# A seven-product feed-forward stage: order of the products and bank copies, GpSimd's subtractions on VectorE, the second group's weights converted ahead through DRAM, conversion steps paced

## The chip, the core and the metric

One NeuronCore of a Trainium2 chip runs the whole program. The metric is the device time of one execution in microseconds; the median of three runs of the kernel before is 1168.42 us.

TensorE (PE) multiplies into eight PSUM banks. VectorE (DVE), ScalarE (ACT) and GpSimd (POOL) do the elementwise work, SyncE (SP) issues the DMAs. Each engine takes its instructions in the order of its own queue, and one that waits holds those behind it.

## The reference

The program chains an attention layer, a gated feed-forward layer and a second feed-forward layer. The change lies in the third:

```python
def _moe2_ref(x, w_in, w_out):          # x: 2304 x 512, w_in: 512 x 2048, w_out: 2048 x 512
    h = np.maximum(x @ w_in, 0.0)
    return (h * h @ w_out).astype(np.float32)

def reference(**kwargs):
    ...
    attn_out = _attn_ref(**attn_kwargs)
    ...
    x = _moe_ref(x=x, **moe_kwargs)     # silu(x @ w_gate) * (x @ w_val) @ w_out, d_ff = 1536
    return _moe2_ref(x=x, **moe2_kwargs)
```

The weights reach the kernel as 64-bit floating-point words. Every operand of a matmul is split into a high part (a copy in the type `fp32r`) and a low part (the difference), and every product is the sum of three matmuls: high by high, high by low, low by high.

## The kernel before

**Stages.** Attention and most of the first feed-forward layer (MoE 1) fill the first 650 us. MoE 1's third group of four f-blocks (`steps2`, `idx == 2`) then runs over five blocks of tokens, four of 512 columns and one of 256. MoE 2 (`steps3`) is last. It has four groups of four f-blocks (`G2`), and each group runs over three sub-blocks `sb` of 768 tokens.

**A sub-block of MoE 2.** `first2` computes the hidden values of one sub-block, `second2` multiplies them by the output weights and adds them into `acc`. `first2` uses a seven-product scheme for two-by-two block matrices: the seven left factors in `LEFT` are sums of blocks of `w_in`, the seven right factors in `FACTORS` are sums of blocks of x. For each of the seven, the two pairs `pr` of f-blocks get six matmuls of 384 columns each, so a product has 12 matmuls. The products accumulate in three pairs of PSUM banks: `A` (mm0, mm1), `Bk` (mm2, mm3) and `C` (mm4, mm5). The line

```python
bank = (A, Bk, A, C, A, A, C)[k][pr][:, :BK]
```

gives the pair of product k. A bank that goes on accumulating is copied out in between: `take` (ScalarE, L1307) copies it into one of three buffers h, `plus` (VectorE, L1310) adds a bank to such a buffer. The next product into the same bank can start only when that read is done. `squares` makes relu(h) squared and splits it into the two halves `u` which `second2` (L1373) reads; on ScalarE that is two instructions (L1298, L1299), on VectorE one (L1296). `second2` runs 72 matmuls of 512 columns.

**The right factors.** `Right2` makes seven factors for each sub-block in five slots of 128 x 1536 elements, ahead of their use. In the first group they are made from x (L1235 subtracts on GpSimd; L53 and L61 are the helpers that make the high copy on ScalarE and the low difference on VectorE), and the four that are sums (`T1` to `T4`) are also stored in DRAM. The later groups load those four and make `11`, `21` and `22` again.

**The weights.** `Weights2` converts the weights of a group. A piece of 128 x 256 words is fetched by SP into one of two buffers `wr`; then come one ScalarE instruction (`absolute`, L1031), four VectorE instructions on integers and floats (L1042, L1045, L1052, L1034), and for each result a high copy on ScalarE (L53) and a low difference on VectorE (L61). The four left factors that are sums take four more VectorE instructions (L1080). A group has 16 pieces, 22 splits and 8 sums. The results go to areas of 128 x 512 ("grains") taken from the list `free`; grains come back when a group's weights were read for the last time. The first group is converted while MoE 1's third group runs, the others each during the group ahead of it.

**What sets the order.** Nothing is ordered by hand on the chip. The generators yield after some matmuls, and `go` then hands out pending copies (`flush`), one step of `Right2` and, by a budget for each engine, some steps of `Weights2` (`turn`). The framework's scheduler takes the instructions in about this order and may move one ahead of another on the same engine.

The names in the rows: `mm` are PSUM banks, `right` and part of `wa` are the slots of the right factors, the rest of `wa` and `wb` hold weights, `wf` and `wr` are the conversion's buffers, `ub` and `wx` hold u, `sum` the sums of `Right2`, `xF` the output sums, `x` is x2.

Of the kernel before, what the change touches and what calls it, by code (L numbers as in the profile page):

```python
# [19 lines left out]
P = 128  # L20
# [47 lines left out]
def attention_moe(tc, qkv, qk0, tau, w1, w2, out, cfg):  # L68
# [902 lines left out]
    class Weights2:  # L971


        def __init__(self):
# [3 lines left out]
            self.raws = {}  # L978
            self.n = 0
            self.used = 0  # L980
            self.turns = 0
            self.touched = {}
            self.fl = [loader.bufs[0][1], loader.bufs[1][1], wf3]
            self.win = {}
            self.wout = {}
            self.left = {}

        def group(self, g):
            for j in range(2):
                f = 4 * g + 2 * j  # L990
                self.wait.append(("in", (g, j), f, 7))
            for j in range(4):
                self.wait.append(("out", (g, j), 4 * g + j, 2))

        def more(self):
            while self.wait and len(self.steps) < 24 and len(free) >= self.wait[0][3]:
                kind, key, f, n = self.wait.popleft()
                area = [free.popleft() for _ in range(n)]
                if kind == "in":
                    self.win[key] = dict(zip(("11", "12", "22", "S1", "S2", "S3", "S4"), area))  # L1000
                    self.pair(key, f)
                else:
                    self.wout[key] = area
                    self.out(key, f)
                self.left[kind, key] = len(self.steps)
# [4 lines left out]
        def fetch(self):  # L1010
            while self.n < self.used + 2 and self.pieces:
                f, c0 = self.pieces.popleft()
                raw = loader.bufs[self.n % 2][0]
                nc.sync.dma_start(raw, w2[f, :, c0 : c0 + PIECE])
                self.n += 1

        def conv(self, f, c0, j):
# [22 lines left out]
            a = ("A", absolute, (j,))  # L1040
# [29 lines left out]
        def pair(self, key, f):  # L1070
            w = self.win[key]

            def sp(j, name):
                return self.split(j, w[name][:, :PIECE], w[name][:, PIECE:], name)
# [27 lines left out]
        def out(self, key, f):  # L1102
            hi, lo = self.wout[key]
            j = 1 + f % 2
            for c in (0, PIECE):
                a, d = self.conv(f, DM + c, j)
                h, l = self.split(j, hi[:, c : c + PIECE], lo[:, c : c + PIECE], "o")
                self.steps += [a, *d, h, l]
                j = 0

        def turn(self):
            self.more()
            self.turns += 1
            budget = {"A": 1, "D": 1 + (self.turns % 4 == 0), "P": 1}
            while self.steps:
                eng, fn, touch = self.steps[0]
                if not budget[eng] or any(
# [5 lines left out]
                budget[eng] -= 1  # L1123

        def emit(self):
            eng, fn, touch = self.steps.popleft()
            for x in touch:
                self.touched[x] = (eng, self.turns)
            fn()

        def until(self, kind, key):
            while any((k, key_) == (kind, key) for k, key_, *_ in self.wait):
                self.more()
                if self.steps:
# [423 lines left out]
```

## Time and profile before

| | |
|---|---|
| median of three runs | 1168.42 us (1167.64 to 1168.72) |
| the profiled execution | 1168.47 us, its span 1166.7 us |
| PE busy | 1120.5 us (96%) |
| weight loads (PEld) busy | 1012.1 us (87%) |
| DVE, ACT, POOL busy | 862.3, 730.1, 268.9 us |
| DMA | 122.19 MB, mean 105 GB/s |

The span runs from the first to the last instruction of the core; 1.77 us of the profiled execution lie around it. Busy times are sums over the whole span, in which stages with different limits follow each other, so the share of an engine says little about one stage. A row of the timeline gives the start of a run of equal instructions, its length, and in brackets how long the engine sat idle ahead of it and which instruction ended that. A row of busy time by stretch gives the stretch, its length, the busy time (and count of instructions) of PE, PEld, DVE, ACT and POOL, then PEclk, the DMA engines' mean busy share and GB/s. The column PEclk gives the granted clock of TensorE as a share of its full 2.4 GHz.

### The profile page before, as it was taken

The numbers are of one execution on the slowest core, as the hardware profiler recorded it, in microseconds if no ns is written. First come the engines' busy times: TensorE is split into PE (matmuls) and PEld (weight loads), VectorE is DVE, ScalarE is ACT, GpSimd is POOL, SyncE is SP. The second block draws the span as 40 slices with busy tenths as digits, with TensorE's granted clock in tenths as the row PEclk, the third lists the DMA queues.
The fourth block names the chain that finished last, engine by engine and source line by source line (L and its number), as shares of the span: only waits on it lengthen the run. The fifth ranks groups of instructions, "written<-read, shape, count | busy, mean of one in ns | idle before, by whom it ended". The sixth has DMA issues, their size and how long they took to land. (4 is left out here: it accounts for less than half of the span.)

```text
span 1166.7 us, 19585 instructions
## 1 busy us (share of the span) xinstructions
PE 1120.5 (96%) x6572; PEld 1012.1 (87%) x6572; DVE 862.3 (74%) x2078; ACT 730.1 (63%) x1734; POOL 268.9 (23%) x377
## 2 busy tenths in 40 slices
PE   6888999999999999999999999989999999999998
PEld 5776989899999999988888888888798898898887
DVE  7999997877777764889976854687678767856443
ACT  7998888988888873555434321255667655655443
POOL 5565664555464521000000000042100000000000
PEclk9999999999999999999999999999999999999999
DMA  6665433344343300233210110133344444333441
GB/s 201 198 167 161 129 101 92 91 119 103 91 115 94 96 2 25 94 91 91 73 56 10 65 36 1 37 117 127 126 145 164 152 136 138 125 120 124 163 163 55
DMA packets 47765, 122.19 MB, mean 105 GB/s; under 512 B 6704, under 2 KB 7984, under 8 KB 47664
## 3 DMA queue, kind: packets, MB, share of 16 engines
q1 hardware_dynamic: 47520, 120.94, 34.4%
q8 instruction: 52, 0.85, 0.3%
q14 instruction: 49, 0.40, 0.1%
q10 hardware_dynamic: 144, 0.00, 0.0%
HBM read 80.22 MB, written 14.16 MB: 81 GB/s over the span
## 5 line engine op out<-in xcount | busy, mean ns | idle before, releaser
L669 PE MATMUL bank<-ident,e 128*128 128x128 f32 x720 | 165.5, 275 | 10.1 <-ACT x L53 3.8
L649 POOL TENSOR_SCALAR e<-e,r 128x576 f32<-128x576 f32 x144 | 113.9, 791 | 147.4 <-DVE r L644 100.9
L61 DVE TENSOR_TENSOR pt<-bank,pt 128x384 fp32r<-128x384 f32 x216 | 100.3, 486 | 51.1 <-ACT pt L689 49.7
L226 PE MATMUL mm<-xs,wa 128*128 128x512 f32 (+2 forms) x672 | 125.8, 347 | 0.5 <-ACT x L53 0.5
L631 ACT ACTIVATE z<-s,thr 128x576 f32<-128x576 f32 x144 | 106.9, 742 | 26.3 <-DVE st__101 L623 18.5
L226 PEld LDWEIGHTS mm<-xs,wa 128*128 128x128 f32 x672 | 109.5, 188 | 15.7 <-ACT x L53 0.7
L623 DVE TENSOR_SCALAR_CACHE_REDUCE st__101<-s,tau_c 128x576 bf16<-128x576 f32 x144 | 116.5, 809 | 4.9 <-PE s L613 3.7
L669 PEld LDWEIGHTS bank<-ident,e 128*128 128x128 f32 x720 | 96.3, 141 | 21.9 <-DVE x L55 5.6
L226 PE MATMUL bank<-xs_m,wa 128*128 128x288 f32 x576 | 109.7, 327 | 3.9 <-DVE xF L740 1.8
L689 ACT ACTIVATE pt<-bank 128x384 fp32r<-128x384 f32 x216 | 88.8, 437 | 21.5 <-PE bank L669 20.2
L639 ACT ACTIVATE e<-z 128x577 f32<-128x577 f32 x144 | 99.6, 691 | 1.5 <-POOL e L649 0.4
L226 PEld LDWEIGHTS bank<-xs_m,wa 128*128 128x128 f32 x576 | 88.9, 189 | 7.3 <-DVE xs_m L61 2.9
L728 PE MATMUL bank<-pt,vs 128*128 128x256 f32 (+1 forms) x480 | 92.2, 323 | 2.1 <-ACT pt L689 1.4
L613 PE MATMUL s<-kh,qs 128*128 128x288 f32 x256 | 78.1, 319 | 7.4 <-ACT nident L413 5.9
L1235 POOL TENSOR_TENSOR sum<-x 128x768 f32<-128x768 f32 x4 | 7.9, 1971 | 315.4 <-DVE wx L61 309.9
L1373 PE MATMUL mm<-wb,ub 128*128 128x512 f32 x324 | 79.4, 394 | 0.0
L1322 PE MATMUL mm<-right,wb 128*128 128x384 f32 x348 | 70.5, 352 | 8.4 <-ACT h L1307 5.0
L728 PEld LDWEIGHTS bank<-pt,vs 128*128 128x128 f32 x480 | 74.0, 190 | 3.9 <-ACT pt L689 2.2
L226 PE MATMUL mm<-xs,wb 128*128 128x512 f32 (+1 forms) x360 | 74.9, 368 | 0.0
L1322 PEld LDWEIGHTS mm<-right,wb 128*128 128x128 f32 x348 | 64.2, 199 | 11.3 <-ACT h L1307 6.6
L613 PE MATMUL s<-kl,qs 128*128 128x288 f32 x256 | 73.7, 301 | 0.0
L226 PEld LDWEIGHTS mm<-xs,wb 128*128 128x128 f32 x360 | 62.8, 188 | 11.3
(157 smaller groups left out, 2602.4 us busy)
## 6 DMA issues: line engine op xcount, KB each, us to landing
wr<-in_w_dram SPq DMA_DIRECT2D x106, 256.0 KB, 3.0
raw<-in_qkv_dram SPq DMA_DIRECT2D x15, 896.0 KB, 4.6
kh<-land SPq DMA_DIRECT2D x60, 144.0 KB, 2.6
kl<-raw SPq DMA_DIRECT2D x60, 144.0 KB, 2.8
xF<-in_w_dram SPq DMA_DIRECT2D x30, 256.0 KB, 3.0
right<-kept0T SPq DMA_DIRECT2D x8, 768.0 KB, 5.4
right<-kept1T SPq DMA_DIRECT2D x7, 768.0 KB, 4.3
right<-kept2T SPq DMA_DIRECT2D x7, 768.0 KB, 5.1
```

What stands on the lines that cost most here:

```text
L61: e.tensor_tensor(out, a, b, op=ALU.subtract)
L226: mm(pt[:, :n], w[:, a, col + c * P : col + (c + 1) * P], xs[:, b, c, :], start=(i == 0), stop=(i == len(TERMS) - 1),)
L613: mm(sp[:, cols], l, r[:, cols], start=(n_ == 0), stop=(n_ == len(pairs) - 1),)
L623: red = nc.vector.tensor_scalar(st_, st[t]["s"][:, :S], scalar1=tau_c, scalar2=None, op0=ALU.subtract, op1=ALU.max, accum_out=th)
L631: nc.scalar.activation(z[:, :S], st[t]["s"][:, :S], AF.Prelu, bias=st[t]["thr"], scale=-1.0, alpha=1 / SLOPE)
L639: ex = nc.scalar.activation(e, st[t]["z"], AF.Exp, scale=-SLOPE, accum_out=sum_)
L649: nc.gpsimd.tensor_scalar(e, e, scalar1=r, scalar2=1.0, op0=ALU.mult, op1=ALU.mult)
L669: mm(dst[:, j], e[:, c0 : c0 + P], ident, is_transpose=True, start=(j == 0), stop=(j == len(cols) - 1),)
L689: nc.scalar.activation(pt[:, s0 : s0 + n, o : o + P], src, AF.Copy)
L728: mm(o[:, :n], hd["vs"][:, SLOT[k % 5], :], pt[:, k, lo : lo + n], start=(k == 0), stop=(k == 9))
L1322: mm(bank, w[:, a, c * P : (c + 1) * P], t[:, b, c, :], start=(n == 0 and x in ("11", "12", "S1")), stop=(n == 5), skip_group_check=x not ...
L1373: mm(pt, u[:, b, s * P : (s + 1) * P], w[a], start=(half == 0 and j == 0 and i == 0), stop=(half == 1 and j == 1 and i == 2),)
```

## The change

1. **Order of products.** The sixth and seventh product change places: `S4` by `22` comes sixth, `22` by `T4` seventh. The banks become A, Bk, A, C, A, C, A. The fourth product (`S1`, bank C) is now copied out by ScalarE, and the fifth (`S3`, bank A) is added to that copy by VectorE; before, it was the other way round. `second2` takes the second half of the token blocks first.
2. **Bank reads early.** `take`, `plus` and the relu reads of a bank are handed to the scheduler with a priority 60 places ahead.
3. **GpSimd idle.** The subtractions of `Right2` run on VectorE.
4. **Squares.** `sq2` chooses the engine by group: VectorE for both pairs in the first and last group, ScalarE in the two between (before: one pair on each in the first group, ScalarE in the rest).
5. **Fifth kept factor.** `22` is stored and loaded again like `T1` to `T4`.
6. **Second group's weights ahead.** All of them are converted right behind the first group's left factors, during MoE 1's third group, into four grains used in turn (`bounce`), stored to DRAM from there, and later loaded into their places.
7. **Pace.** VectorE steps of `Weights2` are handed out by a credit per turn (0.95 in MoE 1, then 0.45 to 1.0) in place of 1.25; the piece behind the current one is fetched as soon as its buffer is free; a piece's first ScalarE step waits 4 turns (8 in MoE 2) from its fetch; freed grains are handed on 8 turns later; `until` flushes no more steps than it needs.

The core of the diff:

```diff
+            ahead = [("ahead in", (1, j), 4 + 2 * j, 0) for j in range(2)]
+            ahead += [("ahead out", (1, j), 4 + j, 0) for j in range(4)]
+            self.wait += left + (ahead + [("given", (1, 0), 0, 0)] if g == 0 else []) + outs
...
+                if kind in ("in", "out") and key[0] == 1:
+                    for x, to in self.win[key].items() if kind == "in" else enumerate(area):
+                        src = keptw[kind, key[1], x]
+                        self.step("S", lambda to=to, src=src: nc.sync.dma_start(to.bitcast(F32), src))
...
+        def store(self, step, to, name):
+            def f():
+                step[1]()
+                nc.sync.dma_start(keptw[name], to.bitcast(F32))
...
-            budget = {"A": 1, "D": 1 + (self.turns % 4 == 0), "P": 1}
+            self.credit = min(self.credit + self.rate, 2)
+            budget = {"A": 1, "D": int(self.credit), "S": 2}
+            while self.later and self.later[0][0] <= self.turns:
+                free.extend(self.later.popleft()[1])
+            self.fetch()
...
+                if raw and self.turns < self.fetched.get(raw[0], self.turns) + self.land:
+                    break
...
-                        free.extend(wbg)
+                        weights2.bounce = deque(wbg[:4])
+                        free.extend(wbg[4:])
...
-    FACTORS = ("11", "21", "T2", "T1", "T3", "T4", "22")
-    LEFT = ("11", "12", "S2", "S1", "S3", "22", "S4")
+    FACTORS = ("11", "21", "T2", "T1", "T3", "22", "T4")
+    KEPT = ("T1", "T2", "T3", "T4", "22")
...
-                        eng.tensor_tensor(out[:, :, c], u, w, op=ALU.subtract)
-
-                return (e, f)
+                        nc.vector.tensor_tensor(out[:, :, c], u, w, op=ALU.subtract)
+
+                return ("D", f)
...
-            e = "DA"[pr] if g == 0 else "A"
+            e = cfg["sq2"][g][pr]
...
+        def read(f, bank):
+            def g_():
+                with tc.high_priority(offset=cfg["soon"]):
+                    f()
+                unread[id(bank)] -= 1
...
-                bank = (A, Bk, A, C, A, A, C)[k][pr][:, :BK]
+                bank = (A, Bk, A, C, A, C, A)[k][pr]
...
                 elif x == "S1":
-                    post = []
+                    post = [take(h[2], bank)]
                 elif x == "S3":
-                    post = [take(h[2], bank), plus(h[2], C[pr][:, :BK]), *squares(pr, 1, 1, h[2])]
+                    post = [plus(h[2], bank), *squares(pr, 1, 1, h[2])]
...
+        order = [*range(nb, 2 * nb), *range(nb)]
...
-                        free.extend(weights2.win[g, pr].values())
+                        weights2.freed(weights2.win[g, pr].values())
...
-    "ta": "P",
+    "sq2": ("DD", "AA", "AA", "DD"),
+    "soon": 60,
+    "pace": (0.95, 0.45, 0.85, 0.55, 1.0),
```

TensorE's queue in the first sub-block of the first group, from the fourth product to the start of `second2` (L1322 and L1381 are `first2`, L1434 is `second2`; the banks are mm0 and mm1 for A, mm4 and mm5 for C). Before:

```order
L1322 MATMUL mm4_6025<-wa_69,wb_5996 128x384 x6
L1322 MATMUL mm5_6026<-wa_69,wb_5996 128x384 x6
L1322 MATMUL mm0_6021<-wa_69,wb_5996 128x384 x6
L1322 MATMUL mm1_6022<-wa_69,wb_5996 128x384 x6
L1322 MATMUL mm0_6021<-right0_8521,wb_5996 128x384 x6
L1322 MATMUL mm1_6022<-right0_8521,wb_5996 128x384 x6
L1322 MATMUL mm4_6025<-right1_8522,wb_5996 128x384 x6
L1322 MATMUL mm5_6026<-right1_8522,wb_5996 128x384 x6
L1373 MATMUL mm6_6027<-wb_5996,ub_6012 128x512 x6
```

Now:

```order
L1381 MATMUL mm4_6025<-wa_69,wb_5996 128x384 x6
L1381 MATMUL mm5_6026<-wa_69,wb_5996 128x384 x6
L1381 MATMUL mm0_6021<-wa_69,wb_5996 128x384 x6
L1381 MATMUL mm1_6022<-wa_69,wb_5996 128x384 x6
L1381 MATMUL mm4_6025<-right0_8671,wb_5996 128x384 x6
L1381 MATMUL mm5_6026<-right0_8671,wb_5996 128x384 x6
L1381 MATMUL mm0_6021<-right1_8672,wb_5996 128x384 x6
L1381 MATMUL mm1_6022<-right1_8672,wb_5996 128x384 x6
L1434 MATMUL mm3_6024<-wa_69,ub_6012 128x512 x3
L1381 MATMUL mm0_6021<-right2_8673,wb_5996 128x384 x6
L1381 MATMUL mm1_6022<-right2_8673,wb_5996 128x384 x6
```

Between two products into mm0 there now always lie 12 matmuls or more into other banks. Three matmuls of `second2` are followed by the next sub-block's first product.

ScalarE's queue around the first `take` of the second sub-block (`h00` from mm0; L1031 is a piece's first conversion step, `wa` from `wf` a weight's high copy). Before:

```order
L53 ACTIVATE xF_64<-mm3_6024 128x512
L1031 ACTIVATE wf22_6004<-wr0_6000 128x256
L53 ACTIVATE wa_69<-wf22_6004 128x256 x2
L53 ACTIVATE xF_64<-mm6_6027 128x512
L53 ACTIVATE wa_69<-wf21_6003 128x256
L53 ACTIVATE xF_64<-mm7_6028 128x512
L1031 ACTIVATE wf20_6001<-wr1_6002 128x256
L53 ACTIVATE wa_69<-wf21_6003 128x256
L1307 ACTIVATE h00_8526<-mm0_6021 128x384
L1307 ACTIVATE h10_8529<-mm1_6022 128x384
```

Now (L1365 is `take`):

```order
L53 ACTIVATE wx_73<-h11_8680 128x384
L53 ACTIVATE ub_6012<-h00_8676 128x384
L53 ACTIVATE right1_8672<-sum0_8674 128x768
L1365 ACTIVATE h00_8676<-mm0_6021 128x384
L53 ACTIVATE wx_73<-h10_8679 128x384
L53 ACTIVATE xF_64<-mm6_6027 128x512
L53 ACTIVATE xF_64<-mm7_6028 128x512
L1365 ACTIVATE h10_8679<-mm1_6022 128x384
L53 ACTIVATE xF_64<-mm2_6023 128x512
```

The conversion's instructions ahead of the `take` are gone, and the `take` stands ahead of the outputs' copies (`xF`).

VectorE's queue at the start of MoE 2 (L286 adds MoE 1's last outputs into `x2b`, L1042 to L1034 are conversion steps, `right` and `wa` from `x2` or `sum` are right factors). Before:

```order
L286 TENSOR_TENSOR x2b_6008<-x2b_6008,mm0_6021 128x256
L61 TENSOR_TENSOR right2_8523<-sum1_8525,right2_8523 128x768
L61 TENSOR_TENSOR wa_69<-wf20_6001,wa_69 128x256
L286 TENSOR_TENSOR x2b_6008<-x2b_6008,mm1_6022 128x256
L61 TENSOR_TENSOR wa_69<-sum0_8524,wa_69 128x768
L1042 TENSOR_SCALAR wf20_6001<-wf20_6001 128x256
L61 TENSOR_TENSOR wa_69<-wf21_6003,wa_69 128x256
L1045 TENSOR_SCALAR wf20_6001<-wf20_6001 128x256
L1052 SCALAR_TENSOR_TENSOR wf20_6001<-wr1_6002,wf20_6001 128x256
L1034 SCALAR_TENSOR_TENSOR wf20_6001<-wr1_6002,wf20_6001 128x256
L1310 TENSOR_TENSOR h00_8526<-mm2_6023,h00_8526 128x384
L61 TENSOR_TENSOR wa_69<-sum0_8524,wa_69 128x768
```

Now (L1281 are the subtractions that GpSimd did, L1368 is `plus`):

```order
L61 TENSOR_TENSOR right0_8671<-x2_65,right0_8671 128x768
L61 TENSOR_TENSOR right1_8672<-x2_65,right1_8672 128x768
L1281 TENSOR_TENSOR sum1_8675<-x2_65,sum0_8674 128x768
L286 TENSOR_TENSOR x2b_6008<-x2b_6008,mm7_6028 128x256
L286 TENSOR_TENSOR x2b_6008<-x2b_6008,mm0_6021 128x256
L286 TENSOR_TENSOR x2b_6008<-x2b_6008,mm1_6022 128x256
L61 TENSOR_TENSOR right2_8673<-sum1_8675,right2_8673 128x768
L61 TENSOR_TENSOR wa_69<-sum0_8674,wa_69 128x768
L1281 TENSOR_TENSOR sum1_8675<-x2_65,sum1_8675 128x768
L1368 TENSOR_TENSOR h00_8676<-mm2_6023,h00_8676 128x384
L1281 TENSOR_TENSOR sum0_8674<-x2_65 128x768
L1368 TENSOR_TENSOR h10_8679<-mm3_6024,h10_8679 128x384
```

Conversion steps have left this place, and subtractions have come.

## Rows read from the trace of the kernel before

**Rows 1.** Busy us (count) by stretch, columns as above: MoE 2's groups, 100 us of MoE 1

```profile
768.94:874.87 105.93, 99.41 (x468) 88.50 (x469) 80.92 (x153) 64.23 (x135) 21.39 (x12) 0.95 0.40 142
874.87:972.82 97.95, 94.55 (x469) 83.93 (x468) 71.65 (x167) 59.98 (x143) 0.00 (x0) 1.00 0.42 142
972.82:1069.35 96.53, 94.12 (x469) 83.98 (x468) 71.51 (x165) 58.09 (x138) 0.00 (x0) 1.00 0.40 137
1069.35:1162.52 93.17, 93.13 (x469) 83.88 (x467) 41.14 (x69) 44.33 (x99) 0.00 (x0) 1.00 0.35 122
660.00:760.00 100.00, 100.00 (x483) 84.56 (x482) 56.20 (x123) 25.93 (x55) 0.00 (x0) 1.00 0.09 30
```

**Rows 2.** Chain of waits (start, length, engine, line): both halves of one sub-block

```profile
1038.35 14.58 PE mm L1322 x84
1052.93 16.58 PE mm L1373 x72
```

**Rows 3.** Who PE waited for from 766 us on: total us, times, longest

```profile
PE mm L1322 <- ACT h L1307: 10.5, 11, 1.5
PE mm L1322 <- DVE h L1310: 1.7, 1, 1.7
PE mm L1322 <- ACT wa L53: 1.5, 1, 1.5
```

**Rows 4.** Timeline of PE: three waits in three groups

```profile
786.17 3.56 PE L1322 MATMUL mm<-right,wb 128*128 128x384 f32 x12 [1.73 <-DVE h L1310]
...
821.86 3.78 PE L1322 MATMUL mm<-right,wb 128*128 128x384 f32 x12 [1.51 <-ACT h L1307]
...
1017.54 2.38 PE L1322 MATMUL mm<-wa,wb 128*128 128x384 f32 x12 [0.69 <-ACT h L1307]
```

**Rows 5.** Three stretches: length, PE busy (count), PEclk, DMA share, GB/s

```profile
770.00:780.00 10.00, 9.87 (x48) 0.83 0.59 236
780.00:790.00 10.00, 7.78 (x36) 0.87 0.34 105
...
820.00:830.00 10.00, 8.49 (x37) 0.83 0.20 79
```

**Rows 6.** Who ACT waited for from 766 us on

```profile
ACT wf L1031 <- DMA wr<-in_w_dram: 31.3, 16, 3.6
ACT wb L53 <- DVE wf L1034: 15.5, 11, 2.1
```

**Rows 7.** Timeline of POOL, one subtraction

```profile
769.74 1.94 POOL L1235 TENSOR_TENSOR sum<-x,sum 128x768 f32<-128x768 f32 x1 [2.42 <-DVE right L61]
```

**Rows 8.** Timeline of DVE, one instruction beside it and three later

```profile
770.25 2.25 DVE L61 TENSOR_TENSOR wa<-sum,wa 128x768 fp32r<-128x768 f32 x1
...
783.37 0.94 DVE L61 TENSOR_TENSOR right<-x,right 128x768 fp32r<-128x768 f32 x1
784.24 0.54 DVE L61 TENSOR_TENSOR wx<-h,wx 128x384 fp32r<-128x384 f32 x1
784.71 0.94 DVE L61 TENSOR_TENSOR wa<-x,wa 128x768 fp32r<-128x768 f32 x1
```

**Rows 9.** Groups (count | busy, mean ns | idle) of DVE, 640 us on

```profile
L1052 DVE SCALAR_TENSOR_TENSOR wf<-wr,wf 128x256 int32<-128x256 int32 x60 | 24.8, 422 | 1.0
...
L61 DVE TENSOR_TENSOR wb<-wf,wb 128x256 fp32r<-128x256 f32 x45 | 18.9, 422 | 14.4 <-PE mm L1322 8.4 <-ACT wb L53 5.6
...
L1042 DVE TENSOR_SCALAR wf<-wf 128x256 f32<-128x256 f32 x58 | 16.3, 290 | 27.6 <-ACT wf L1031 27.3
```

**Rows 10.** Group of ACT, same stretch: the conversion's high copies

```profile
L53 ACT ACTIVATE wb<-wf 128x256 fp32r<-128x256 f32 x45 | 18.5, 414 | 38.1 <-DVE wf L1034 23.0 <-PE mm L1322 11.4 <-DVE wf L1080 3.6
```

**Rows 11.** DMA issues, same stretch: count, KB each, median us to landing

```profile
wr<-in_w_dram SPq DMA_DIRECT2D x58, 256.0 KB, 3.1
right<-kept0T SPq DMA_DIRECT2D x8, 768.0 KB, 5.4
...
out_dram<-xF SPq DMA_DIRECT2D x18, 256.0 KB, 2.0
```

More of the change, by code (lines that the diff above doesn't have):

```diff
@@ L978, in __init__ @@
             self.raws = {}
+            self.fetched = {}
+            self.land = 4
+            self.later = deque()
             self.n = 0
@@ L982, in __init__ @@
             self.touched = {}
+            self.credit = 0
+            self.emitted = 0
+            self.last = {}
+            self.rate = cfg["pace"][0]
             self.fl = [loader.bufs[0][1], loader.bufs[1][1], wf3]
@@ L999, in more @@
                 if kind == "in":
-                    self.win[key] = dict(zip(("11", "12", "22", "S1", "S2", "S3", "S4"), area))
-                    self.pair(key, f)
-                else:
-                    self.wout[key] = area
-                    self.out(key, f)
-                self.left[kind, key] = len(self.steps)
+                    self.win[key] = dict(zip(LEFT, area))
+                elif kind == "out":
+                    self.wout[key] = area
+                if kind in ("in", "out") and key[0] == 1:
+                    for x, to in self.win[key].items() if kind == "in" else enumerate(area):
+                        src = keptw[kind, key[1], x]
+                        self.step("S", lambda to=to, src=src: nc.sync.dma_start(to.bitcast(F32), src))
+                elif kind == "in":
+                    self.pair(self.win[key], f)
+                elif kind == "out":
+                    self.out(area, f)
+                elif kind == "given":
+                    self.step("S", lambda: free.extend(self.bounce))
+                else:
+                    names = LEFT if kind == "ahead in" else range(2)
+                    w = {}
+                    for x in names:
+                        w[x] = self.bounce[0]
+                        self.bounce.rotate(-1)
+                    (self.pair if kind == "ahead in" else self.out)(w, f, kind[6:], key[1])
+                self.last[kind, key] = self.emitted + len(self.steps)
         def step(self, eng, fn, *touch):
@@ L1013, in fetch @@
                 raw = loader.bufs[self.n % 2][0]
+                self.fetched[self.n] = self.turns
                 nc.sync.dma_start(raw, w2[f, :, c0 : c0 + PIECE])
@@ L1107, in out @@
                 h, l = self.split(j, hi[:, c : c + PIECE], lo[:, c : c + PIECE], "o")
+                if kind and c:
+                    for x in range(2):
+                        l = self.store(l, w[x], (kind, j_, x))
                 self.steps += [a, *d, h, l]
@@ L1129, in emit, with freed @@
             fn()
+        def freed(self, grains):
+            self.later.append((self.turns + 8, list(grains)))
         def until(self, kind, key):
-            while any((k, key_) == (kind, key) for k, key_, *_ in self.wait):
+            while (kind, key) not in self.last or self.emitted < self.last[kind, key]:
+                if not self.steps and self.wait and len(free) < self.wait[0][3]:
+                    free.extend(self.later.popleft()[1])
                 self.more()
-                if self.steps:
-                    self.emit()
-                else:
-                    assert self.wait and len(free) >= self.wait[0][3]
-            while self.steps:
-                self.emit()
+                self.emit()
+    LEFT = ("11", "12", "S2", "S1", "S3", "S4", "22")
+    dram = p2.enter_context(tc.tile_pool(name="dram", bufs=1, space=bass.MemoryType.DRAM))
+    keptw = {
+        (kind, j, x): dram.tile([P, 2 * PIECE], F32, name=f"kept_{kind}{j}{x}")
+        for kind, n, names in (("in", 2, LEFT), ("out", 4, range(2)))
+        for j in range(n)
+        for x in names
+    }
     weights2 = Weights2()
```

72 lines of the change are left out of this document (39 added, 33 removed).

## The prediction, made blind

> **What bounds the kernel now.** I read the busy time by stretch first, to find where TensorE is not full. Up to MoE 2 it is: 100.00 of 100 us between 660 and 760 us, at full clock [rows 1]. MoE 2's four groups do the same matmuls, and take 105.93, 97.95, 96.53 and 93.17 us [rows 1]. The last has no wait: a sub-block is 14.58 us of products and 16.4 to 16.6 us of output matmuls [rows 2], and three of them make the 93.17. So TensorE's own work is the bound, and the change touches no matmul. What is there to win is 12.76 + 4.78 + 3.36 = 20.9 us above the last group's time, and the wait of 1.5 us ahead of the first product [rows 3]: **22.4 us**. Without them the profiled execution, 1168.47 us, would be 1146.1 us.
>
> Then I read who TensorE waited for. The list from 766 us on has 13 waits, 13.7 us, 10.5 us of them on `take` (L1307) in 11 places [rows 3]. Six of these stand ahead of the sixth product, as in [rows 4] at 821.86 us and 1017.54 us: before, it goes into bank A right behind the fifth, so ScalarE has only the other pair's 1.04 us (six of the 84 matmuls of [rows 2]) for the copy. The six are 0.49 to 1.51 us long and sum to 4.7 us. The other five (5.8 us) stand at the third or fifth product, where the bank was left alone for 3.1 us: there the copy was late because ScalarE's queue was held. The list of ScalarE's waits says by what: 31.3 us on fetched words and 15.5 us on VectorE's part of the conversion [rows 6].
>
> The clock costs a second piece. In three stretches of 10 us it is 0.83, 0.87 and 0.83 [rows 5], so TensorE ran part of them at its lower level, 1.2 of 2.4 GHz, and lost 1.7 + 1.3 + 1.7 = 4.7 us. It fell behind idle gaps of 1.5 us and more: the 1.5 us ahead of the stage [rows 3], 1.73 us at 786 and 1.51 us at 821 [rows 4]; in the second and third group, whose waits were shorter, it stayed at 1.00 [rows 1]. The last 4.0 us of the 22.4 are the refill behind each wait and gaps under the list's threshold.
>
> **The change part by part.**
>
> *Order of products and early reads.* Behind each product into a bank there now lie at least 12 matmuls into other banks, plus the other pair's six: 18 x 0.174 = 3.1 us for a copy, everywhere. The six waits of 4.7 us go. Copies and additions are as many as before. In ScalarE's queue the conversion's instructions no longer stand ahead of the first `take` of the second sub-block.
>
> *Second group's weights ahead.* A group is 16 pieces, 22 splits, 8 sums: on VectorE 16 x (2 x 0.29 + 2 x 0.42) + 30 x 0.42 = 35 us, on ScalarE 38 x 0.42 = 16 us [rows 9, 10]. They leave the first group, whose VectorE was busy 80.92 of 105.93 us, and go into the 115 us of MoE 1's third group, where VectorE was busy 56.20 of 100 and ScalarE 25.93 [rows 1]. 56 + 31 = 87 of 100 fits. What covers it there: a hidden block's values are read by an output product two units (10.9 us of matmuls) later (48 of them by 16.4 / 72 = 0.23 us). New there are 22 stores of 256 KB, and a grain is written again only after its store. A store of 256 KB lands in 2.0 us, one of 768 KB or its load in up to 5.4 [rows 11]. Four grains take turns, so only the last split of a pair comes directly behind the store of its own grain: two holds of ScalarE by 2.0 to 5.4 us, hidden by the 10.9. I take 0. In the built order all these steps, and the first group's own output weights, stand ahead of the first product.
>
> *GpSimd's subtractions on VectorE.* One takes GpSimd 1.94 us [rows 7]; the VectorE instruction beside it took 2.25 us where the same shape takes 0.94 later [rows 8]. So each of the 14 cost VectorE up to 1.3 us already, about 18 us in all, and as VectorE's own they cost 10 x 0.87 + 4 x 0.47 = 10.6 us (distance of starts in [rows 8]). The tight place is the first sub-block. From the built order VectorE has there nine instructions of 768 elements, eleven of 384 and one of 256 beside 14.58 us of products: 9 x 0.87 + 11 x 0.47 + 0.3 = 13.2 us. It fits, with 1.4 us to spare. Followed one by one: the first factors are ready when MoE 1's last output bank is added, some 0.3 us behind its last matmul (the wait of 1.5 us goes), and none of the seven factors is late. The first late thing is the sixth product's u for the output half: VectorE reaches its square 2.7 us behind the last product, ScalarE's copy of it stands behind three factor copies, and TensorE, with 3.1 us of other matmuls put in by the scheduler, waits **0.85 us**.
>
> The Trainium skill (Perfetto Trace Analysis, section Optimizing Scalar/DVE Operations) speaks against this part: it says that GpSimd and VectorE share a read port, so that moving work between them might not help. By that the first group would keep half of its loss (1156 us, the first rival); by the rows the moved instructions cost VectorE less than the collisions did. The Trainium skill's page SBUF — State Buffer (section SBUF: two separate sides) agrees with the rows: the loser of the port is blocked for the other's whole instruction.
>
> *Squares on VectorE in groups one and four.* 0.47 us there for two instructions on ScalarE. In the last group VectorE was busy only 41.14 of 93.17 us [rows 1]. The output half now starts with the token blocks of the sixth product, whose u has 3.1 us plus up to 0.7 us of filler matmuls. Its chain (add, square, copy, low part) is some 2.0 us, behind a queue of other squares. Bounds per handover: 0 and the 0.85 of the first. I take 0.2 for the eleven others, nearer to 0 because the copies of factors that stood in the first one's way are loads in groups two to four: **2.2 us**.
>
> *Factor `22` through DRAM.* Nine loads of 768 KB, up to 5.4 us [rows 11], each issued when its slot is free (2.1 us into the products) and needed 8.3 us later. Hidden; 3 us are left. They free VectorE and ScalarE of a copy and a subtraction per sub-block.
>
> *Pace and earlier fetch.* ScalarE's 31.3 us on fetched words [rows 6] should mostly go: a sub-block's products are 28 turns, so 8 turns are some 4 us, and a piece lands in 3.1 [rows 11]. Groups two and three still convert, so something stays: bounds 0 and the 8.1 us that both lost, less their sixth-product waits (2.7 us). I take **1.0 us**.
>
> Sum: 1146.1 + 0.85 + 2.2 + 1.0 = **1150.1 us** in terms of the profiled execution, which stands 0.05 us above the median of the runs shown: 1150.0.
>
> **The rivals.**
>
> *VectorE becomes the bound of the first group.* For it: only 1.4 us to spare in the first sub-block, and every stall of 1.5 us there would take the clock down, as it did twice. Against it: 35 us of conversion have gone from this group. It would then keep about half of its 12.76 us: 6 us more, **1156 us**. By the Trainium skill's sentence above on the shared port this would be the likelier end.
>
> *Conversion still holds ScalarE in groups two and three.* A fetch stands in SP's queue behind factor loads that wait for TensorE, so a piece can land later than the pace supposes. Then these groups keep their 8.1 us, 1150.1 - 1.0 + 8.1 = **1157 us**.
>
> *No change.* The waits only move: the scheduler's new order (products of the next sub-block among output matmuls) could put TensorE behind factors that are not ready, as often as it waited before: 1166 to 1171, say **1168 us**.
>
> *Slower: the work moved into MoE 1 is not hidden.* Place: ScalarE's queue between 650 and 767 us, where words to fetch and 22 stores are waited for, with the tanh of MoE 1 queued behind. If a store comes back late (above 5.4 us), each split waits for it. 22 x 2.0 = 44 us of holds come together at the row's price. It decides once more than the 22.4 us that are won reaches TensorE, half of them: 1150 + 22 = **1172 us**. Against it: the full 100 us of TensorE [rows 1] with ScalarE busy a quarter, and 10.9 us of cover.
>
> **How the numbers follow.** Forecast (1146.5 to 1154): 0.66. VectorE bound, 1154 to 1160: 0.15. ScalarE still held, 1154 to 1160: 0.10. No change: 0.04. Slower: 0.05. The range 1146 to 1160 holds the first three but for their edges, rather more than 8 in 10, since its lower end is a floor and its upper end belongs to two rivals. A measurement of this kernel can tell about 0.2% (2.3 us) from no change; faster by more than that 0.91, within it 0.04, slower 0.05.
>
> **What would show it.** In the changed kernel's busy time by stretch TensorE should stay full up to MoE 2, and the four groups take 93 to 96 us each. The list of TensorE's waits should have no entry at the sixth or seventh product, and short ones (under 1 us) at the first matmuls of the output half. PEclk should be 1.00 throughout MoE 2, and the VectorE instructions of 768 elements 0.94 us each. Wrong would be: a first group above 98 us (VectorE), waits on `take` in groups two and three (ScalarE), idle TensorE or a clock below 1.00 between 650 and 767 us (the moved work), or waits on loads of `right`.

## The result and the profile after

The changed kernel takes 1158.22 us (median of four runs, 1156.49 to 1159.01), the kernel before beside it 1168.57 us; the ratio is 0.991 with a 95% interval of 0.9893 to 0.9927. It is faster by 10.35 us. The forecast was 1150.0 us in a range of 1146 to 1160, so sign and range hold, and some 8 us of the forecast gain are missing. The profiled execution took 1159.01 us.

Busy time by stretch of the changed kernel, MoE 2's four groups and three stretches around its start (stretch, length, busy and count of PE, PEld, DVE, ACT, POOL, PEclk, DMA share, GB/s):

```profile
773.68:868.57 94.89, 93.82 (x472) 84.48 (x471) 63.60 (x113) 48.28 (x91) 0.00 (x0) 1.00 0.52 191
868.57:963.88 95.31, 93.32 (x467) 83.59 (x466) 65.49 (x150) 55.61 (x133) 0.00 (x0) 1.00 0.47 162
963.88:1059.49 95.61, 94.13 (x470) 83.84 (x468) 66.68 (x155) 55.10 (x133) 0.00 (x0) 1.00 0.47 161
1059.49:1153.36 93.87, 93.83 (x469) 83.97 (x467) 49.10 (x90) 26.10 (x54) 0.00 (x0) 1.00 0.42 146
...
750.00:760.00 10.00, 10.00 (x62) 8.99 (x62) 7.04 (x21) 2.90 (x8) 0.00 (x0) 1.00 0.23 81
760.00:770.00 10.00, 6.76 (x39) 6.15 (x38) 7.75 (x18) 4.42 (x9) 0.00 (x0) 0.76 0.51 176
770.00:780.00 10.00, 10.00 (x62) 10.00 (x61) 7.69 (x14) 4.47 (x8) 0.00 (x0) 0.90 0.61 196
```

The groups that took 105.93, 97.95, 96.53 and 93.17 us [rows 1] take 94.89, 95.31, 95.61 and 93.87 us. MoE 2 as a whole is 379.7 us, where the prediction's floor and its three additions make 376.7. But it begins at 773.68 us. Before, it began at 768.94, behind a wait of 1.5 us [rows 3], so without that wait at 767.4: 6.3 us are lost ahead of the stage, at the end of MoE 1. There the clock, full before, is at 0.76 and 0.90.

Who PE waited for from 640 us on, in the changed kernel (total us, times, longest):

```profile
PE mm L1434 <- ACT ub L53: 3.9, 4, 2.0
PE mm L271 <- ACT wx L53: 3.2, 2, 1.6
PE mm L1381 <- ACT h L1407: 0.6, 1, 0.6
```

All 11 waits on `take` and the one on `plus` [rows 3] are gone. New are two waits of MoE 1's output matmuls (L271), 3.2 us. The timeline of PE shows them, and the two longest of MoE 2:

```profile
763.92 0.96 PE L271 MATMUL mm<-wx,wa 128*128 128x256 f32 x3 [1.56 <-ACT wx L53]
766.49 0.58 PE L271 MATMUL mm<-wx,wa 128*128 128x256 f32 x1 [1.60 <-ACT wx L53]
...
792.62 3.06 PE L1434 MATMUL mm<-wa,ub 128*128 128x512 f32 x12 [1.06 <-ACT ub L53]
...
885.42 3.03 PE L1434 MATMUL mm<-wb,ub 128*128 128x512 f32 x12 [1.99 <-ACT ub L53]
```

Both gaps at 764 and 766 us end with a high copy of MoE 1's hidden values (`wx` from `k_th`). The timeline of ScalarE tells what held it (L1053 is a piece's first conversion step, L246 the tanh of MoE 1):

```profile
759.54 0.44 ACT L1053 ACTIVATE wf<-wr 128x256 f32<-128x256 f32 x1 [0.58 <-DVE wb L61]
759.88 0.37 ACT L246 ACTIVATE k_th<-mm 128x256 f32<-128x256 f32 x1
763.14 0.43 ACT L1053 ACTIVATE wf<-wr 128x256 f32<-128x256 f32 x1 [2.88 <-DMA wr<-in_w_dram]
763.47 0.40 ACT L53 ACTIVATE wx<-k_th 128x256 fp32r<-128x256 f32 x1
763.77 0.37 ACT L246 ACTIVATE k_th<-mm 128x256 f32<-128x256 f32 x1
766.02 0.42 ACT L53 ACTIVATE wx<-k_th 128x256 fp32r<-128x256 f32 x1 [1.88 <-DVE k_th L256]
766.56 0.44 ACT L1053 ACTIVATE wf<-wr 128x256 f32<-128x256 f32 x1
```

The second first-step of a piece (L1053) waited 2.88 us for its words; the copy of hidden values, whose input VectorE had ready at 761.70 us, stood behind it, and so did the tanh of the next unit (L246). Behind the waits the matmuls are slow: the mean clock of 0.76 and 0.90 in two stretches of 10 us is 2.4 and 1.0 us lost at the lower level. From the first output matmul of the last block (761.48 us) to MoE 2 are 12.2 us here, and 5.99 us in hold_third below: 3.2 us of waits, and 3.0 us that I put down to the slower matmuls, near the 3.4 us that the clock gives.

These three pieces (759.54, 763.14, 766.56 us) are not work of this place at all. In ScalarE's queue 32 first steps stand ahead of them, the 16 pieces of the first group and the 16 of the second, so they are the first three pieces of the third group's weights. The program hands them out when the second group begins (868 us); the scheduler put them about 100 us earlier. I take the reason to be that they wait for nothing but the conversion's own buffers; no run shows the reason itself.

### The profile page after: what moved, and what is told of

The parts are those of the page before. It is cut to its first block, busy times and chain, and to the rows that moved or that the text cites. A ratio compares the mean times of both kernels' runs of the same rounds, so it can differ in the third digit from the quotient of the medians.

```text
span 1157.2 us, 19662 instructions
## 1 busy us (share of the span) xinstructions
PE 1117.7 (97%) x6572; PEld 1010.6 (87%) x6572; DVE 865.9 (75%) x2119; ACT 701.6 (61%) x1662; POOL 242.6 (21%) x363
## 4 chain that ended last, share of the span: by engine, by line
PE 69%; DVE 15%; ACT 8%; issue 3%; DMA 3%; POOL 0%; POOLq 0%; DVEq 0%; ACTq 0%; SPq 0%
PE mm L226 17%; PE mm L1434 14%; PE mm L1381 10%; PE mm L271 8%; PE bank L226 6%; PE bank L669 4%; PE bank L271 4%; PE s L613 3%; PE bank L728 3%; DMA wr<-in_w_dram 3%; DVE st__101 L623 3%; DVE pt L61 1%; ACT z L631 1%; ACT e L639 1%; ACT h L1349 1%
## 5 line engine op out<-in xcount | busy, mean ns | idle before, releaser
L1451 DVE TENSOR_TENSOR xF<-xF,mm 128x512 f32<-128x512 f32 x54 | 36.9, 686 | 50.5 <-PE mm L1434 50.2
L1365 ACT ACTIVATE h<-mm 128x384 f32<-128x384 f32 x72 | 34.7, 485 | 57.0 <-PE mm L1381 56.6
L1053 ACT ACTIVATE wf<-wr 128x256 f32<-128x256 f32 x64 | 27.5, 433 | 65.5 <-DMA wr<-in_w_dram 51.1
L1434 PE MATMUL mm<-wb,wx 128*128 128x512 f32 x270 | 67.1, 389 | 0.0
```

The costliest lines, as they stand in the source:

```text
L1434: mm(pt, u[:, b, s * P : (s + 1) * P], w[a], start=(half == 0 and j == 0 and i == 0), stop=(half == 1 and j == 1 and i == 2),)
```

## Experiments

Theory A: these pieces, which hold ScalarE, are the missing time. Theory B: the loads of kept weights, which stand in SP's queue and wait for TensorE, make the fetches late. Theory C: VectorE has too much to do at the end of MoE 1.

**The three pieces held back** (hold_third):

```diff
-                nc.scalar.activation(fl, words()[1].bitcast(F32), AF.Abs)
+                with tc.issue_after(marks[0]) if 32 <= k < 35 else ExitStack():
+                    nc.scalar.activation(fl, words()[1].bitcast(F32), AF.Abs)
```

`k` numbers the pieces, 16 to a group; `marks[0]` is the first copy of a bank in the first group's third sub-block.

> The changed kernel with one edit: the first ScalarE instruction of the three pieces of the third group, which the scheduler had put between the last copies of hidden values of MoE 1, must stand behind the first copy of a bank in the third sub-block. Theory A (ScalarE is held there by these pieces, 2.88 us of waiting for words at 763 us, with the copies of hidden values behind it): MoE 2 begins at 767.5 to 768.5 us in place of 773.7, the clock is 1.00 between 760 and 780 us, and the time falls by 5 to 7 us to 1151 to 1153 us. Theory B (the loads of kept weights in SP's queue make every fetch late): MoE 2 begins at 771 us or later, since the words of the first group's own output weights are late all the same. Theory C (VectorE has too much to do at the end of MoE 1): no change, 1158 us.

Measured: 1151.55 us, ratio 0.9856 (0.9842 to 0.9871), 6.7 us less than the changed kernel. MoE 2 begins at 768.06 us. Busy time by stretch of this kernel, around the start and in the first group:

```profile
760.00:770.00 10.00, 10.00 (x79) 9.87 (x78) 8.12 (x15) 4.56 (x8) 0.00 (x0) 1.00 0.46 159
770.00:780.00 10.00, 10.00 (x59) 10.00 (x58) 9.68 (x16) 7.16 (x13) 0.00 (x0) 1.00 1.00 384
768.06:862.87 94.81, 93.75 (x472) 84.47 (x471) 65.70 (x122) 49.10 (x94) 0.00 (x0) 1.00 0.53 197
```

Its ScalarE at the same place:

```profile
758.57 0.36 ACT L246 ACTIVATE k_th<-mm 128x256 f32<-128x256 f32 x1
760.10 0.42 ACT L53 ACTIVATE wx<-k_th 128x256 fp32r<-128x256 f32 x1 [1.16 <-DVE k_th L256]
760.83 0.38 ACT L246 ACTIVATE k_th<-mm 128x256 f32<-128x256 f32 x1 [0.31 <-PE mm L226]
762.72 0.42 ACT L53 ACTIVATE wx<-k_th 128x256 fp32r<-128x256 f32 x1 [1.51 <-DVE k_th L256]
```

The copies now wait for their own data only, TensorE and its clock are full, and VectorE, busier in both stretches than in the changed kernel (8.12 and 9.68 against 7.75 and 7.69 us), is no hindrance. That is theory A to its number, and against C. The edit takes these pieces' VectorE steps out of the place as well, so it shows that the pieces are the cause, not that ScalarE's queue alone was.

**Kept weights loaded by GpSimd's queue** (loads_on_gpsimd):

```diff
-    self.step("S", lambda to=to, src=src: nc.sync.dma_start(to.bitcast(F32), src))
+    self.step("S", lambda to=to, src=src: nc.gpsimd.dma_start(to.bitcast(F32), src))
```

> The changed kernel with one edit: the loads of the second group's kept weights are issued by GpSimd, which is idle there, and no longer by SP, so no fetch of words stands behind a load that waits for TensorE. Theory A (the three pieces are in ScalarE's queue where they don't belong): a fetch lands at most 1 us earlier, 1156 to 1158 us. Theory B (SP's queue makes them late): the wait of 2.88 us at 763 us falls under 1 us, MoE 2 begins at 767.5 to 769 us, 1151 to 1154 us. Theory C (VectorE): 1158 us.

1156.26 us (0.9896, 0.9881 to 0.9911). ScalarE's wait of 2.88 us is still 2.31 us, MoE 2 begins at 773.08 us, and the two gaps in the timeline of PE stay:

```profile
764.57 0.96 PE L271 MATMUL mm<-wx,wa 128*128 128x256 f32 x3 [1.57 <-ACT wx L53]
766.80 0.52 PE L271 MATMUL mm<-wx,wa 128*128 128x256 f32 x1 [1.28 <-ACT wx L53]
```

B falls as the cause of these. What it gains, 2.0 us with overlapping intervals, fits the wait at 885 us, which is 0.62 us here; there ScalarE's stand of 1.48 us for words (881.12 us in the changed kernel) is gone, so B has a small part in MoE 2. With both edits together (hold_loads_gpsimd) nothing is added:

> Both edits in one kernel: the three pieces held back as in hold_third, and the loads of the second group's kept weights issued by GpSimd. The wait of 1.99 us at 885 us was 0.62 us with either edit alone, so together they should give nothing more: 1150.5 to 1152 us, MoE 2 from 767.5 to 768 us, four waits of 0.3 to 1.1 us. Were SP's queue a cause of its own, 1149 us or less.

1151.31 us (0.985, 0.9835 to 0.9865), as hold_third.

**A longer time from fetch to first step** (land_12):

```diff
-            self.land = 4
+            self.land = 12
```

> The changed kernel with one number changed: in MoE 1 a piece's first ScalarE step waits 12 turns from its fetch in place of 4. In the built order no piece of the third group then stands ahead of the last copies of hidden values, and one pair of the first group's output weights is converted in the first sub-block. Theory A: MoE 2 begins at 767.5 to 769 us; the first output half waits up to 1 us more for its weights or its hidden values; 1151 to 1154 us. Theory B: as A, since each fetch has longer to land. Theory C (VectorE's amount of work): 1157 to 1159 us, since the same steps are there.

1152.94 us (0.9873, 0.9856 to 0.989), MoE 2 from 767.3 us. The number moved the pieces out of the place by another road, as A has it. B forecast the same here, so this run speaks against C alone.

**Without the weights converted ahead** (no_ahead):

```diff
-(ahead + [("given", (1, 0), 0, 0)] if g == 0 else [])
+([("given", (1, 0), 0, 0)] if g == 0 else [])
...
-                if kind in ("in", "out") and key[0] == 1:
+                if False:
```

> The changed kernel without its sixth part: the second group's weights are converted during the first group again, with neither stores nor loads of kept weights; all other parts as they are. Theory A: MoE 1 ends within 2 us of the kernel before (MoE 2 begins at 767.5 to 769.5 us), and the first group takes 97 to 101 us, since 35 us of VectorE's steps are back beside 74 us of its other work in 95 us, and pieces stand in ScalarE's queue again; 1155 to 1160 us. If the part is worth what the prediction says, the first group loses at least 4 us against the 94.9 us of the changed kernel. Theory C (the moved volume is what MoE 1 loses): MoE 2 begins at 767.5 us, and the first group is about as long as now, 1152 us.

1154.48 us (0.9882, 0.9867 to 0.9897): 3.7 us less than the changed kernel, and 2.9 us more than hold_third. So the sixth part cost time as it stood, and is worth some 3 us once the three pieces are kept out of MoE 1. Its first group takes 95.4 us (767.33 to 862.71) and not the 97 to 101 that I expected; it has two waits on `u` (1.06 and 0.29 us), and the others stand in the second and third. Conversion beside the first group's own work does little harm, which made me doubt my account of where the 12.76 us of before had come from.

**GpSimd's subtractions.** First put back into hold_third (hold_gpsimd_sums):

```diff
-                        nc.vector.tensor_tensor(out[:, :, c], u, w, op=ALU.subtract)
+                        nc.gpsimd.tensor_tensor(out[:, :, c], u, w, op=ALU.subtract)
```

> The kernel hold_third (1151.55 us) with the 14 subtractions of the right factors on GpSimd again. By the rows of before, each costs VectorE up to 1.3 us while it runs there and 0.47 to 0.87 us as VectorE's own, so the first group should get longer, and its first sub-blocks above all: VectorE's instructions of 768 elements above 2 us beside them, 2 to 6 us more, 1153 to 1158 us. If moving them between the two engines is worth nothing, the time stays at 1151 to 1152 us.

1163.88 us (0.9961, 0.9946 to 0.9976): 12.3 us more from 14 instructions, more than the 6 us that I thought possible. VectorE in this kernel, an instruction beside GpSimd's, one alone and one beside GpSimd's longest, and then GpSimd:

```profile
765.21 2.60 DVE L61 TENSOR_TENSOR right<-x,right 128x768 fp32r<-128x768 f32 x1
...
768.39 0.94 DVE L61 TENSOR_TENSOR right<-sum,right 128x768 fp32r<-128x768 f32 x1
...
790.84 0.94 DVE L61 TENSOR_TENSOR right<-sum,right 128x768 fp32r<-128x768 f32 x1
```

```profile
764.55 2.44 POOL L1282 TENSOR_TENSOR sum<-x,sum 128x768 f32<-128x768 f32 x1
...
790.12 4.77 POOL L1282 TENSOR_TENSOR sum<-x,sum 128x768 f32<-128x768 f32 x1 [7.36 <-DVE wa L61]
```

In one meeting VectorE loses (2.60 us in place of 0.94), in the other GpSimd (4.77 us, while VectorE keeps its 0.94), and TensorE waits (who PE waited for from 640 us on):

```profile
PE mm L1441 <- ACT ub L53: 6.9, 7, 1.6
PE mm L1388 <- DVE x2b L286: 1.8, 2, 1.5
PE mm L1388 <- ACT h L1368: 1.3, 3, 0.8
```

Then the same word changed in the kernel before, and nothing else (before_vector_sums):

```diff
-    "ta": "P",
+    "ta": "D",
```

> The kernel before with one word changed: the subtractions of the right factors run on VectorE and no longer on GpSimd. Theory D (GpSimd's subtractions, each of which slows VectorE while it runs, were the larger part of the first group's loss of 12.76 us; putting them back cost hold_third 12.3 us): the first group falls from 105.9 to 96 to 99 us, its clock to 0.98 or more, and the time to 1159 to 1163 us. Theory E (they matter only beside the new squares on VectorE; the first group of before was held by conversion and by the order of the products): 1165 to 1169 us.

1155.87 us, ratio 0.9885 (0.9864 to 0.9906): 13.4 us, more than the whole change. Busy time of its four groups, and who PE waited for from 640 us on:

```profile
767.81:861.23 93.42, 93.42 (x470) 84.08 (x469) 77.40 (x166) 64.38 (x136) 0.00 (x0) 1.00 0.43 161
861.23:958.88 97.65, 94.48 (x469) 83.93 (x468) 71.55 (x168) 60.09 (x143) 0.00 (x0) 1.00 0.42 143
958.88:1055.02 96.14, 94.26 (x470) 84.13 (x469) 71.38 (x164) 58.09 (x138) 0.00 (x0) 1.00 0.39 138
1055.02:1148.01 92.99, 92.97 (x469) 83.72 (x467) 41.12 (x69) 44.35 (x99) 0.00 (x0) 1.00 0.34 122
```

```profile
PE mm L1322 <- ACT h L1307: 5.1, 7, 1.4
```

The first group falls from 105.93 to 93.42 us and TensorE has no wait in it at all, with the old order, the old banks, the old pace, and the second group's conversion still in it. VectorE is busy for 77.40 of 93.42 us, before for 80.92 [rows 1], though it has the subtractions now. The 1.5 us ahead of the stage are gone too. The second and third group are as they were (97.95 and 96.53 [rows 1]), with seven waits on `take`. The run changes two things at once: the two engines no longer meet, and a subtraction takes 0.95 us on VectorE in place of 1.94 on GpSimd, with no handing over between engines. How much of the 13.4 us is which wasn't separated.

This bears on the Trainium skill's two pages, which the prediction set against each other. Perfetto Trace Analysis (section Optimizing Scalar/DVE Operations) says that moving work between GpSimd and VectorE might not help, since they share a read port; here moving it took 13.4 us off, so the warning does not hold for this case. SBUF — State Buffer (section SBUF: two separate sides) says that the loser of the shared port waits for the other's whole instruction; the 2.60 us beside GpSimd, which end 0.82 us behind the end of GpSimd's instruction, agree.

**The order of products and banks.** Alone, in the kernel before (before_new_order):

```diff
-                bank = (A, Bk, A, C, A, A, C)[k][pr][:, :BK]
+                bank = (A, Bk, A, C, A, C, A)[k][pr][:, :BK]
...
-                    post = []
+                    post = [take(h[2], bank)]
...
-                    blk, s = divmod(s0 + e, nb)
+                    blk, s = divmod(order[s0 + e], nb)
```

> The kernel before with the first part of the change alone: the new order of products and banks, the new reads of the fourth and fifth product, the new order of the token blocks in the output half. As the prediction has it, six waits of 4.7 us and two of the three stretches at a lower clock (1.3 and 1.7 us) go: 1161 to 1164 us. If the order is worth as little as in hold_old_order (0.8 us), the waits on the copies of banks come at other products: 1166 to 1170 us.

1172.24 us, ratio 1.0027 (1.0018 to 1.0037): slower. Who PE waited for from 640 us on:

```profile
PE mm L1374 <- ACT ub L53: 7.5, 7, 1.6
PE mm L1322 <- DVE h L1310: 3.1, 4, 1.6
PE mm L1374 <- DVE wx L61: 2.8, 2, 1.5
PE mm L1374 <- DVE ub L61: 2.2, 2, 1.3
PE mm L1322 <- ACT wa L53: 1.5, 1, 1.5
PE mm L1322 <- ACT h L1307: 0.5, 2, 0.3
```

The waits on `take` fall from 10.5 to 0.5 us, as predicted, and 12.5 us of waits on u come up at the output half (L1374), which begins with the token blocks of the sixth product, as it did before. The sixth is now the one whose u needs an addition by VectorE first, and some of VectorE's instructions are slowed beside GpSimd's (a square of 128 x 384 takes 2.20 us at 793.35 us, and 0.55 at 786.24). I take these two together for the cause; no run parts them. Whether the order would have helped beside VectorE's sums in the kernel before wasn't tried.

Undone in hold_third (hold_old_order: old order, banks, reads and order of token blocks):

```diff
-                bank = (A, Bk, A, C, A, C, A)[k][pr]
+                bank = (A, Bk, A, C, A, A, C)[k][pr]
...
-        order = [*range(nb, 2 * nb), *range(nb)]
+        order = [*range(2 * nb)]
```

> The kernel hold_third with the old order of the sixth and seventh product, the old banks (A, Bk, A, C, A, A, C), the old reads of the fourth and fifth product and the old order of the token blocks in the output half; the priority of the bank reads stays. If the 12 matmuls between two products into one bank are what took the waits away, the waits at the sixth product come back, eleven or twelve of 0.5 to 1.5 us, and in the first group the clock falls behind them: 1157 to 1164 us. If the waits on copies of banks were only ScalarE's queue held by conversion (which is paced now), the time stays within 2 us, 1151 to 1154 us.

1152.37 us (0.9854, 0.9838 to 0.987): the same as hold_third. Then the early reads undone as well (hold_old_order_late_reads):

```diff
-    "soon": 60,
+    "soon": 0,
```

> The kernel hold_old_order (1152.37 us) with the priority of the bank reads taken away too, so that the first two parts of the change are undone together. If the priority is what made the old order harmless, the waits at the sixth product come back, eleven of 0.5 to 1.5 us, 1157 to 1163 us. If neither counts once GpSimd is idle and conversion is paced, 1151 to 1154 us.

1156.82 us (0.989, 0.9873 to 0.9907), 4.5 us more. The first waits on `take` are in the second group, and in all there are:

```profile
PE mm L1387 <- ACT h L1368: 7.1, 7, 1.9
```

With the early reads that entry is, in hold_old_order:

```profile
PE mm L1387 <- ACT h L1368: 1.8, 3, 0.6
```

So the priority of the bank reads is what the second and third group needed, with the old order of products. Whether the new order would have done without the priority in hold_third wasn't tried.

**Pace and squares.** Without the pacing of MoE 2 (hold_no_pace), and with the old engines for the squares (hold_old_squares):

```diff
-    "pace": (0.95, 0.45, 0.85, 0.55, 1.0),
+    "pace": (0.95, 1.25, 1.25, 1.25, 1.25),
...
-        weights2.land = 8
+        weights2.land = 0
```

> The kernel hold_third with the pacing of MoE 2 taken away: 1.25 steps of VectorE per turn in each part of a group in place of 0.45 to 1.0, and no turns between a fetch and a piece's first ScalarE step. If the pacing is what took the waits away in the second and third group (97.95 and 96.53 us before), they come back there, with ScalarE waiting some 30 us for words: 1154 to 1159 us. If the order and the early reads did it, 1151 to 1153 us.

1151.34 us (0.9845, 0.9828 to 0.9861): nothing. ScalarE waits 14.6 us for words from 766 us on, against 13.4 in hold_third and 31.3 before [rows 6]. The earlier fetch, the pace in MoE 1 and the later return of grains were still in, and no run undoes them, nor the fifth kept factor.

```diff
-    "sq2": ("DD", "AA", "AA", "DD"),
+    "sq2": ("DA", "AA", "AA", "AA"),
```

> The kernel hold_third with the old choice of engines for the squares: in the first group one pair on each engine, in the last group both on ScalarE. The prediction priced this part at nothing by itself. In the last group ScalarE has 44 us of work in 93, so it should stay at 93 to 94 us; in the first, ScalarE's queue gets six instructions more per sub-block, and the first wait of the output half (1.06 us) can grow to 1.5 us: 1151 to 1153 us.

1150.89 us (0.9848, 0.9833 to 0.9862): nothing that can be told from hold_third, and the first output half's wait of 1.06 us is gone rather than grown.

hold_third and its four variants at 1150.9 to 1152.4 us are faster than both kernels, and not to be told from each other.

## Why the prediction was right, and where not

**The floor and the bound were right.** TensorE's own work sets the end: with GpSimd idle a first group takes 93.42 us of unbroken matmuls (before_vector_sums), near the 93.17 of the last [rows 1]. MoE 2 in hold_third, 377.7 us (768.06 to 1145.72), stands 1 us above the 376.7 of the sum. The list of waits of the changed kernel is near what was foretold: one of 0.6 us at the products, the others at the output half, though two of these are above the 1 us foretold (1.06 and 1.99). The one of 0.6 us shows that the rule of 12 matmuls between two products into one bank has an exception: in the queue shown ahead of the prediction only nine lie between the seventh product into mm0 and the next sub-block's first, and there TensorE waited at 1011.67 us for the read of that bank (L1407). The clock is 1.00 from 780 us on.

**The handover was sized well**: 0.85 us foretold for the first sub-block, 1.06 measured at that place; 2.2 us for the eleven others, 1.4 us in the list of hold_third (0.62, 0.33 and 0.47), and 2.8 in the changed kernel, with the wait of 1.99 us.

**The step that failed in the sum is "Second group's weights ahead", taken at 0.** As changed, it costs 3.7 us (1158.22 against 1154.48 without it). Two things were wrong in its working. The cover of 10.9 us belongs to blocks of 512 columns with another unit between; in the last block, of 256 columns, TensorE asks for the hidden values at once (the gap ahead of 763.92 us begins at 762.36, 0.7 us after VectorE finished them). And I counted the steps that the change moves there, and overlooked that the scheduler puts the next free steps, those of the third group, behind them. ScalarE's queue shows it: two of the three L1053 stand ahead of the last two copies of hidden values, the third right behind them. The sign named beforehand for a failure of this step, idle TensorE and a clock below 1.00 just ahead of 767 us, is the one that showed. The rival for "slower" named the place and the queue, but not these pieces, and its price was for stores.

**That the range holds is in part luck.** 1158.22 us lies outside the forecast's own 1146.5 to 1154, in the 1154 to 1160 that the prediction gave to two rivals, VectorE as the bound of the first group and ScalarE held in groups two and three. The first did not come: the first group takes 94.89 us. Of the second one wait is seen, the 1.99 us at 885.42 us, behind a stand of ScalarE of 1.48 us for words at 881.12 us. Most of the time was lost at a third place, ahead of MoE 2.

**Two steps had the wrong cause and a total that came out.** I gave the waits at the sixth product to the order of products, since they stood behind six matmuls of the other pair, and the other waits on `take` to the conversion in ScalarE's queue. The kernel before with VectorE's sums has the same order and the same conversion, and none of these waits in its first group: 1.04 us is enough for a copy where ScalarE comes on time. GpSimd's subtractions were priced as 18 us of VectorE's time against 10.6, a gain of cover. They were the whole of the first group's loss, 12.5 us of group time and the 1.5 us ahead of the stage. The rows for that were in front of me [rows 7, 8]: I summed the engine's time and didn't follow the chain to the factors. And the pace of MoE 2, which was to leave 1.0 of 5.4 us (8.1 less 2.7), was worth nothing by itself; the early reads, which I didn't price by themselves, 4.5 us. That MoE 2 came within 3 us of its sum all the same is luck as far as these causes go: whichever part takes a wait away, the floor is the same.

Two small readings of the prediction are off and decide nothing: VectorE's work in the first sub-block adds up to 13.3 us, not 13.2, and the 5.4 us of [rows 11] are a median, not an upper bound.

**By parts**: VectorE's sums alone take 13.4 us off, to 1155.87. All the other parts but the sixth add little to that: no_ahead, which has them, is at 1154.48 us, and the two intervals overlap (0.9867 to 0.9897 and 0.9864 to 0.9906). The weights ahead give 3 us more when their neighbours are held back (without that part the second group has waits of 0.82 and 1.68 us, with it one of 0.62), and cost 3.7 as they stand. The 4.5 us of the early reads were measured with the weights ahead in place and the old order; the parts overlap, and what they are worth does not add up. The order, the squares and the pace of MoE 2, each undone in hold_third, can't be told from nothing.

## What to carry to other kernels

Where two engines disturb each other, change that one assignment alone before rewriting the order around it: one word in the kernel before was worth more than seven parts together. Price each part beside the others too, since two parts can remove the same wait. When work is moved to an earlier stage, read in the built order what the scheduler puts behind it there, and look for instructions of much later steps that wait for a fetch ahead of copies that TensorE needs. A wait that goes at one product can come back at the next consumer; the list of waits by line shows it at once.

## What was unexpected of the hardware

A subtraction of 128 x 768 on GpSimd beside VectorE's work took up to 4.77 us (790.12 us in hold_gpsimd_sums) where most take 1.8 to 2.5, while VectorE's instruction of 768 elements beside it (790.84 us) kept its 0.94. At 765 us of the same kernel it was VectorE's that took 2.60. Either engine can be the one that loses, one of them in each of these two meetings.

The clock doesn't follow the length of a gap alone. It fell behind gaps of 1.56 and 1.60 us at 764 and 766 us in the changed kernel, and behind 1.73 us in the kernel before [rows 4, 5]. But the longest gap of the changed kernel, 1.99 us at 885.42 us, left it at 1.00 (busy time by stretch of that kernel):

```profile
880.00:890.00 10.00, 8.01 (x40) 6.76 (x39) 7.91 (x21) 7.89 (x20) 0.00 (x0) 1.00 0.86 284
```

In before_new_order a gap of 1.62 us at 785.51 us, with several more in the same 20 us, left it at 1.00 as well (busy time by stretch):

```profile
780.00:790.00 10.00, 6.78 (x37) 5.68 (x35) 9.97 (x15) 6.58 (x13) 2.20 (x2) 1.00 0.32 114
790.00:800.00 10.00, 7.66 (x31) 5.70 (x32) 9.97 (x18) 6.33 (x14) 5.06 (x3) 1.00 0.46 186
```

So the prediction's reading, that the clock falls behind gaps of 1.5 us and more, holds for the kernel before and not in general. What tells these cases apart stays open.
